# Start of a fused attention and gated-MLP kernel: state loads placed first, five weight loads fetched at once, and two sign steps moved

## Chip, cores, metric

One core of one Trainium2 chip. The metric is the time of one execution in microseconds (us), several executions each; "span" is the same execution as the profiler sees it, some 1.8 us shorter. This is a program on one core, so no other core's clock plays a part.

## The reference

```python
def _attn_ref(x, state):            # x (8, 8, 512, 64), state (8, 8, 32, 64), float32
    scores = scale * x @ state^T;  softmax -> a;   xread = a @ state
    scores2 = scale * state @ x^T; softmax -> a2;  sread = a2 @ x
    return concatenate([xread, sread], axis=2)

def _moe_ref(x, w_in, w_out):       # x (4608, 512) after the bridge; w_in (512, 2048)
    h = x @ w_in
    return (h * cos(h)) @ w_out
```

(`^T` and the softmax line are shortened.) The weights arrive as 64-bit floats. The kernel loads them raw and converts them on the chip; a good part of its first 125 us is this conversion.

## The kernel before: what the change touches

The start loads the first batch's x (eight loads, one per head) and half of the state, and asks for the first three weight loads. The two hardware queues are those of SP (`nc.sync`) and ScalarE (`nc.scalar`); Pool (`nc.gpsimd`) has the software queue.

```python
    def load_x(b, queues):
        src = x[b].rearrange("h (c p) d -> p c h d", p=P)
        for h in range(H):
            queues[h % 2].dma_start(out=x_b[:, :, h], in_=src[:, :, h])
    # ... cut ...
    load_x(0, (nc.sync, nc.scalar))
    # ... cut ...
    load_state(0, (nc.scalar, nc.gpsimd))      # eight loads of 32 KB, four each
    # ... cut ...
    fetch(3)                                   # weight loads 0, 1, 2, 512 KB each
    load_state(1, (nc.sync, nc.sync))
    warm(2, at[0])
    a0 = attn[0] = Attention(0)
    a0.all_tokens()                            # 16 transposes of x, four copies
    states(0, at[0])                           # 4 transposes of the state
    states_kept(0, at[0])
    a0.scores()
    warm(6, acc[SIDE][1])                      # matmuls nobody reads
    convert(0, "12ab")
    convert(1, "12a")
    a0.max1()                                  # two L305 reductions
    a0.spread1()
    a0.shift()
    a0.exp1()
    convert(0, "cd")
    convert(1, "bcd")
    a0.sums()
    a0.spread1()
    convert(2, "12")
    a0.norm1()
    # ... products, max2, exp2, then the regular steps, each a hidden tile with a gate
```

One weight load is converted in six steps. "1" and "2" are ScalarE's (the high and the low word as float), "a" and "b" are VectorE's (Pool does "a" of load 1). "c", the **sign step**, is VectorE's L226: it takes two operands from SBUF and frees the raw data. "d" is Pool's sum (L236). Raw data sits in three slots, and load n + 3 waits until load n's "c" is through.

## Time and profile before

| kernel before | us |
|---|---|
| time, median of six executions | 821.08 (820.25 to 821.51) |
| last x load landed | 8.4 |
| last state load of the first half landed | 12.39 |
| first weight load landed | 9.8 |
| first reduction of max1 began | 16.54 |
| norm1 ended | 27.45 |
| copy of the first gate (L445) began | 31.88 |
| first L389 of the stage's end (below: "stage end") | 121.64 |
| TensorE holds the path from about | 125 |

Terms: a load has *landed* when its completion is recorded. max1, exp1, sums and norm1 are the steps of the first softmax, max2 and exp2 the start of the second; the *gate* is h * cos(h) of a hidden tile, and its first step copies h. TensorE's clock is called *cold* where only half of it was granted (0.50) and *warm* at the full one (1.00).

The landings are from the trace's records of each load's completion, the landmarks below them from the chain of waits and the timeline. The lines of the chain are in the prediction.

### The profile page before, as it was taken

Reading aid. Unit: us, or ns where it says so; the run is one execution under the profiler, and the core shown is the slowest. Engines: PE = TensorE matmul, PEld = TensorE weight load, DVE = VectorE, ACT = ScalarE, POOL = GpSimd, SP = SyncE. Lnnn points to the kernel's source line nnn. Section 1 sums busy time; section 2 is a strip of 40 time slices with the busy share of each in tenths; the row PEclk is TensorE's granted clock in tenths of the full one; section 3 lists DMA queues with packets and bytes.
Section 4 is the critical chain, followed back from the end, with each engine's and each line's share of the span. In section 5 each row is a group of like instructions: output and inputs, shape, how many; then the busy total and the mean of one; then the engine's idle time right before and its main releaser. Section 6 shows DMA issues by size and latency. Waiting matters only on the chain.

```text
span 818.6 us, 7603 instructions
## 1 busy us (share of the span) xinstructions
PE 779.7 (95%) x2736; PEld 349.9 (43%) x2736; DVE 435.0 (53%) x671; ACT 397.6 (49%) x644; POOL 184.0 (22%) x135
## 2 busy tenths in 40 slices
PE   6788788989999999999999999999999999999997
PEld 3233234334434443444444344444344444455554
DVE  3899897653355435863454456743554355432431
ACT  2667775554447444644455444634473445322222
POOL 2244237876100000154000000451000002620200
PEclk7899999999999999999999999999999999999999
DMA  6575350101000211030010211120000112100021
GB/s 154 180 213 178 123 155 1 26 8 45 1 15 12 52 26 26 13 65 0 1 26 7 58 23 16 33 46 0 14 14 0 27 26 54 75 1 13 14 38 38
DMA packets 111653, 37.19 MB, mean 45 GB/s; under 512 B 103616, under 2 KB 103616, under 8 KB 111616
## 3 DMA queue, kind: packets, MB, share of 16 engines
q1 hardware_dynamic: 108800, 35.93, 18.1%
q10 hardware_dynamic: 2688, 0.66, 0.4%
q8 instruction: 21, 0.34, 0.2%
q0 software_dynamic: 128, 0.13, 0.1%
q14 instruction: 16, 0.13, 0.1%
HBM read 27.79 MB, written 8.91 MB: 45 GB/s over the span
## 4 chain that ended last, share of the span: by engine, by line
PE 78%; DVE 11%; ACT 7%; issue 1%; DMA 1%; POOL 0%; ACTq 0%; DVEq 0%; POOLq 0%
PE o L504 42%; PE h L439 25%; PE at L291 4%; PE o L621 3%; DVE q L448 2%; PE at L378 2%; ACT q L454 1%; PE at L264 1%; DVE g_all L460 1%; ACT q L453 1%; DVE xT L311 1%; DVE aT L355 1%; ACT xT L337 1%; DVE w_in L226 1%; DVE w_in L221 1%
## 5 line engine op out<-in xcount | busy, mean ns | idle before, releaser
L439 PE MATMUL h<-aT,sw 128*128 128x512 f32 x512 | 247.8, 607 | 16.4 <-DVE g_all L460 11.9
L504 PE MATMUL o<-g_all,w_out 128*128 128x512 f32 x512 | 238.7, 603 | 4.5 <-DVE sw L418 2.9
L466 POOL TENSOR_TENSOR g_all<-g_all 128x512 f32<-128x512 f32 x80 | 112.0, 1421 | 460.7 <-DVE g_all L460 455.7
L445 ACT ACTIVATE q<-h 128x512 f32<-128x512 f32 (+1 forms) x144 | 82.2, 571 | 270.2 <-PE h L439 270.2
L448 DVE SCALAR_TENSOR_TENSOR q<-q,h 128x512 f32<-128x512 f32 (+1 forms) x144 | 94.2, 654 | 208.8 <-ACT q L445 208.8
L504 PE MATMUL o<-g_all,s 128*128 128x512 f32 x384 | 177.3, 598 | 0.0
L460 DVE TENSOR_TENSOR g_all<-h,q 128x512 f32<-128x512 f32 (+1 forms) x144 | 94.8, 658 | 139.5 <-ACT q L454 139.3
L439 PEld LDWEIGHTS h<-aT,sw 128*128 128x128 f32 x512 | 98.0, 194 | 145.5 <-issue 112.1
L504 PEld LDWEIGHTS o<-g_all,w_out 128*128 128x128 f32 x512 | 93.9, 190 | 127.1 <-issue 120.6
L453 ACT ACTIVATE q<-q 128x512 f32<-128x512 f32 (+1 forms) x144 | 87.5, 608 | 103.7 <-DVE q L448 103.7
L504 PEld LDWEIGHTS o<-g_all,s 128*128 128x128 f32 x384 | 70.3, 190 | 88.4 <-issue 83.6
L454 ACT ACTIVATE q<-q,halfpi 128x512 f32<-128x512 f32 (+1 forms) x144 | 100.5, 698 | 4.5
L236 POOL TENSOR_TENSOR w_out<-w_out,s 128x512 int32<-128x512 int32 x20 | 27.2, 1379 | 84.8 <-DVE w_out L226 80.0
L466 DVE TENSOR_TENSOR g_all<-g_all 128x512 f32<-128x512 f32 x48 | 33.2, 692 | 1.6
L439 PE MATMUL h<-sT,w_in 128*128 128x256 f32 x128 | 30.2, 379 | 0.0
L236 POOL TENSOR_TENSOR w_in<-w_in,s 128x512 int32<-128x512 int32 x16 | 21.7, 1369 | 37.7 <-DVE w_in L226 37.7
L420 ACT COPY sw<-at 128x512 f32<-128x512 f32 x48 | 25.7, 588 | 9.0 <-PE at L291 9.0
L621 PE MATMUL o<-w_out,g_all 128*128 128x512 f32 x64 | 29.6, 592 | 0.0
L439 PEld LDWEIGHTS h<-sT,w_in 128*128 128x128 f32 x128 | 24.3, 190 | 10.1 <-issue 6.7
L510 DVE SCALAR_TENSOR_TENSOR held<-o,held 128x512 f32<-128x512 f32 x40 | 25.4, 681 | 3.7 <-PE o L504 3.7
L291 PE MATMUL at<-w_in,stT 64*32 64x512 f32 x384 | 26.1, 601 | 0.0
L531 DVE STREAM_TRANSPOSE ot<-held 128x512 f32<-128x512 f32 x32 | 22.2, 694 | 0.0
(84 smaller groups left out, 472.5 us busy)
## 6 DMA issues: line engine op xcount, KB each, us to landing
out_dram<-ot SPq DMA_DIRECT2D x136, 64.0 KB, 2.0
g_all<-in_moe_w_out_dram SPq DMA_DIRECT2D x8, 1024.0 KB, 5.0
x_b<-in_x_dram SPq DMA_DIRECT2D x60, 128.0 KB, 2.9
g_all<-in_moe_w_in_dram SPq DMA_DIRECT2D x6, 1024.0 KB, 5.2
g_all<-in_moe_w_in_dram SPq DMA_DIRECT2D x4, 512.0 KB, 5.6
x_b<-in_moe_w_out_dram SPq DMA_DIRECT2D x1, 1024.0 KB, 5.7
xT<-in_moe_w_out_dram SPq DMA_DIRECT2D x1, 1024.0 KB, 7.8
x_b<-in_x_dram ACTq DMA_DIRECT2D x4, 128.0 KB, 4.7
```

Source lines behind the costliest of these rows:

```text
L236: nc.gpsimd.tensor_tensor(bits[:, r], bits[:, r], e.bitcast(I32)[:, r], op=ALU.add)
L291: nc.tensor.matmul(out=(to or at)[j][Ns * k:Ns * k + Ns, 0:n], lhsT=w[D * j:D * j + D, self.b, Ns * k:Ns * k + Ns], rhs=r(slice(D * j, D * ...
L420: nc.scalar.copy(dst, to[j][:, 0:c1 - c0])
L439: nc.tensor.matmul(out=t.hp, lhsT=t.lhs(i), rhs=t.rhs(i), start=(i == 0), stop=(i == t.kn - 1))
L445: nc.scalar.activation(t.q, t.hp, func=ACTF.Copy, bias=MAGIC)
L448: nc.vector.scalar_tensor_tensor(out=t.q, in0=t.q, scalar=MAGIC, in1=t.hp, op0=ALU.subtract, op1=ALU.subtract)
L453: nc.scalar.activation(t.q, t.q, func=ACTF.Abs)
L454: nc.scalar.activation(t.q, t.q, func=ACTF.Sin, bias=halfpi, scale=-TWO_PI)
L460: nc.vector.tensor_tensor(t.g, t.hp, t.q, op=ALU.mult)
L466: engine.tensor_tensor(out, a, b, op=ALU.subtract)
L504: nc.tensor.matmul(out=acc[bank][ch], lhsT=w[:, i, P * ch:P * ch + P], rhs=g.g, start=(i == 0), stop=(i == NH - 1))
L621: nc.tensor.matmul(out=acc[MAIN][i], lhsT=t.g[:, P * i:P * i + P], rhs=w_out[:, :, t.f, :], start=(n == 0), stop=(n == NF - 1))
```

## The change

Its intent: put the state first on its queue, as the scores waited for it; have the weights in early; and keep two VectorE steps away from Pool's use of the same memory.

```diff
-    load_x(0, (nc.sync, nc.scalar))
+    load_x(0)                    # all eight on nc.sync
@@ fetch: places of the raw data
-                at_ = n_fetched % 3
+                at_, c0 = (n_fetched - 2) % 3, 0
+                if n_fetched < 4:     # loads 0..3: two halves of two slots
+                    at_, c0 = n_fetched // 2, n_fetched % 2 * 2 * m * w
@@ convert
-        if "c" in parts and i + 3 < N_LOADS:
-            fetch(i + 4)
+        if "c" in parts and i not in (1, 2) and i + 3 < N_LOADS:
+            fetch(max(i + 4, 6))
-        e = low[i % 2][:, 0:m * w]...
+        c0 = m * w if i in (2, 3) else 0
+        e = low[i % 2][:, c0:c0 + m * w]...
@@ start
-    fetch(3)
+    fetch(5)
-    a0.all_tokens()
+    a0.all_tokens(0, 3)
     states(0, at[0])
     states_kept(0, at[0])
+    a0.all_tokens(3, 4)
     a0.scores()
-    warm(6, acc[SIDE][1])
+    warm(7, acc[SIDE][1])
@@
-    convert(0, "cd")
     convert(1, "bcd")
     a0.sums()
+    convert(0, "cd")
```

(Cut: the new arguments of `all_tokens` and the call for later batches. The changed kernel's lines are numbered four or so higher: L305 becomes L309, L226 becomes L230, L445 becomes L449.)

More of the change, by code (lines that the diff above doesn't have):

```diff
@@ L102, with load_x @@
     stT = consts.tile([P, B, P], F32)
-    def load_x(b, queues):
+    def load_x(b):
         src = x[b].rearrange("h (c p) d -> p c h d", p=P)
         for h in range(H):
-            queues[h % 2].dma_start(out=x_b[:, :, h], in_=src[:, :, h])
+            nc.sync.dma_start(out=x_b[:, :, h], in_=src[:, :, h])
     zeros = g_all[:, 0]
     nc.vector.memset(zeros, 0.0)
-    load_x(0, (nc.sync, nc.scalar))
+    load_x(0)
     st_src = state.rearrange("b (k j) n d -> j k n b d", j=2)
@@ L181, in fetch @@
                 m, w = dst.shape[1:]
-                at_ = n_fetched % 3
+                at_, c0 = (n_fetched - 2) % 3, 0
+                if n_fetched < 4:
+                    at_, c0 = n_fetched // 2, n_fetched % 2 * 2 * m * w
                 if n_fetched >= N_LOADS:
                     at_ = 3 + n_fetched - N_LOADS
-                raw = raw_at[at_].bitcast(I32)[:, 0:2 * m * w]
+                raw = raw_at[at_].bitcast(I32)[:, c0:c0 + 2 * m * w]
                 raw = raw.rearrange("p (m f) -> p m f", m=m)
@@ L211, in convert_part @@
         m, w = dst.shape[1:]
-        e = low[i % 2][:, 0:m * w].rearrange("p (m f) -> p m f", m=m)
+        c0 = m * w if i in (2, 3) else 0
+        e = low[i % 2][:, c0:c0 + m * w].rearrange("p (m f) -> p m f", m=m)
         if p == "1":
@@ L273, in tokens_kept, with all_tokens @@
             nc.scalar.copy(self.xT[:, k], at[k % 2])
-        def all_tokens(self):
+        def all_tokens(self, k0, k1):
             xp = [acc[k // 2][k % 2] for k in range(NK)]
-            for k in range(NK):
+            for k in range(k0, k1):
                 for c in range(NC):
@@ L429, in part @@
         if (name, args) == ("reads", (1,)) and b + 1 < B:
-            load_x(b + 1, (nc.sync, nc.sync))
+            load_x(b + 1)
     class Tile:
```

## The prediction

> **What bounds the kernel now.** I read the page first: the busy digits by slice, then the chain that ended last.
>
> ```profile
> PE   6788788989999999999999999999999999999997
> ...
> DVE  3899897653355435863454456743554355432431
> ...
> PEclk7899999999999999999999999999999999999999
> ```
>
> One slice is 20.5 us. TensorE stands at 90% or more from the ninth slice on; in slices 2 to 6 VectorE is the fuller one. So the kernel is a start, a VectorE-bound stage to about 125 us, and then TensorE to the end. The changed lines are all in the first 30 us. They leave the work behind that alone, so what they can give is one constant shift. I therefore read the chain of waits over the first 32 us in order of time (columns: start us, length us, what):
>
> ```profile
> 1.85 5.22 DMA x_b<-in_x_dram
> ...
> 7.09 0.32 ACTq L123
> ...
> 7.45 4.94 DMA s<-in_state_dram
> ...
> 12.52 1.10 PE at L138 x4
> ...
> 14.49 2.06 PE at L291 x16
> 16.54 1.31 DVE m L305 x2
> ...
> 20.44 0.60 DVE w_in L226
> 21.04 0.35 DVE w_in L223
> ...
> 21.41 1.65 DVE w_in L226
> 23.06 1.23 DVE m L305 x2
> ...
> 26.22 1.23 DVE aT L355
> ...
> 31.88 0.49 ACT q L445
> ```
>
> The path to the scores (L291) is not x but the state: ScalarE's queue issues four x loads and only then its four state loads, and these come late. The timeline of the first 60 us gives the issues:
>
> ```profile
> 0.72 2.21 ACTq L108 DMA_DIRECT2D x_b<-in_x_dram  x4
> ...
> 4.18 3.71 ACTq L123 DMA_DIRECT2D s<-in_state_dram  x4
> ...
> 8.43 0.66 PE L264 MATMUL o<-ident,x_b 128*128 128x128 f32 x4 [0.66 <-DMA x_b<-in_x_dram]
> ...
> 12.52 1.09 PE L138 MATMUL at<-ident,s 128*128 128x128 f32 x4 [3.43 <-DMA s<-in_state_dram]
> ```
>
> Its 3.71 us for four issues of about 0.35 us are waits: eight completion semaphores go round the two hardware queues, and each state load waits for an x load that holds its semaphore. The last one waits for the x load that landed at about 7.1, is issued at 7.45 and lands at 12.39, behind 512 KB weight loads in the same engines. The last x was there at 8.4, so TensorE stood idle 3.43 us for the state alone, then ran the transposes and scores on a cold clock (1.00 of the clock granted in 0 to 5 us, 0.50 in 10 to 15).
>
> **What the Trainium skill says.** "DMA: Bandwidth & Descriptors", section "Issuing engines are not separate DMA queues": loads of all issuers run on the same 16 engines and interleave; issuing from several only saves issue time. The trace agrees: an ACT state load of 32 KB took about 4.9 to 6.7 us to land here, while the SP state loads issued from 9 to 14 us have a median of 2.3. "SBUF — State Buffer", section "Who interferes with whom": a VectorE operation with two SBUF inputs contends with a GpSimd operation that reads SBUF, a reduction does not. The trace agrees: one sign step (L226, 128x512) took 0.68 us alone and 1.65 us beside Pool's sum of 21.12 to 22.50, and the L305 reductions took 1.29 us for two beside the next Pool sum, against 1.31 without. "ScalarE: Activation LUTs", section "What ACT_TABLE_LOAD costs": about 1283 ns for the load; the trace has 1.28 us at 7.92, between ScalarE's last issue and its first copy. "TensorE: Matmul & The Clock Gate", section on the clock gate: half clock after an idle window of some 3.4 us; the trace's half-clock transposes at 12.52 (0.42 us mean against 0.27) follow such a gap.
>
> **The change, part by part.**
>
> *State first, x on SP alone.* ScalarE now issues its four state loads at once, from 0.7, without a wait. They should land at about 3.0 to 4.5 (2.3 us for such a load in a quiet stretch, some more behind x). Pool's four are as before; the last was issued at 3.3 and landed at about 8.6 and I take 8.0 now, as one hardware queue competes with it instead of two. SP issues eight x loads: four at 0.5 us each to 2.8, then one after each landed holder of its semaphore (first state about 3.1, first x about 4.0, second state, second x about 4.7), so the last goes out at about 5.0 and, at 3 to 3.4 us, lands at about 8.3. Bytes agree: x landed at one 128 KB load per 0.55 us in the quiet stretch, and ten such units (x and half the state) from 2.9 make 8.4. So x is no earlier; the state no longer adds 4 us. With the state's transposes ahead of the last of x: state transposed 8.0 to 8.7, last x 8.7 to 9.35, its copy (0.69) to 10.1, scores of the last head pair end at about 10.5. Before: 16.5. The table load goes to about 2.3, out of the way.
>
> *Weights.* Their loads now stand behind all of x on SP. The first is issued at about 5.5 instead of 3.77 and lands after x at about 9.8 (512 KB at the 300 to 340 GB/s of the weights' stretches is some 1.6 us; before it landed at about 9.8 also), the second at about 11.5 (before 11.9). The first conversion is ahead of the maxima in VectorE's order: ScalarE 9.85 to 10.5, VectorE's two steps (0.42 + 0.43) to 11.45. That, not the scores, becomes the wait: max1 starts at 11.5 instead of 16.52. **Gain 5.0 us.** Loads four and five were issued at 21.1 and 23.1 and used at 25.75 and 32.25 with no wait for a DMA named in the timeline, so having them early is worth nothing by itself; the loads afterwards keep their distance.
>
> *Sign steps.* Before, from the end of shift (20.44) to the start of sums (23.0) VectorE ran 0.68 + 0.42 + 1.65 us. Now exp1 (1.06 on ScalarE) covers the second load's two steps (0.43 + 0.69, Pool idle), sums start 1.1 us after shift, and the first load's sign step (0.69) stands after them, when Pool's sum (1.3) is over. So 2.55 becomes 1.1 + 0.7 = 1.8: **gain 0.75 us**. VectorE's norm1 ends at 11.5 + (27.45 - 16.52) - 0.75 = 21.7, 5.75 earlier. The other branch: Pool's sum of the first load starts at about 19.2, ends 20.5; 16 products (1.3) and two copies (0.65) make the first weights of the hidden layer at 22.6, against 27.59 when hidden started: 5.0 earlier only. It now comes after norm1 and is the later wait of the first hidden tile. But the tile's gate at 31.77 waited for VectorE's max2 and ScalarE's exp2, not for it: h needs 1.7 to 3.3 us from 22.6, to at most 25.9, and exp2 would end at about 26.1. So the shift of the gate is about 5.6.
>
> *A seventh warm-up matmul* adds 0.43 to 0.9 us to TensorE while it would wait for Pool: nothing on the path.
>
> Sum: 5.0 + 0.75 less 0.15 for joints = 5.6 us. Everything after is released by the work before it, with no clock of its own, so I carry it whole: 821.1 - 5.6 = 815.5; I add 0.3 for what the VectorE stage may lose in new overlaps with Pool. **815.8 us**.
>
> **Rivals.** (1) *The wait moves to the weights.* If x and the first weights fill the engines more than I count, the first 512 KB lands at 11.5 to 12 instead of 9.8; max1 then starts at about 13.5 and the gain is 3.5: 817.6. For it: the weights have lost 1.7 us at issue, and 3 MB of weights are now asked for at once. Against it: within a queue the first weights stand ahead of the rest, and x moved at only some 235 GB/s, which leaves issue and latency as the limit. (2) *Pool's sum of the first load becomes the path*: if h is later than exp2, the gain is 5.0 or less, to 816.2 or so; speaking for it is a cold TensorE, against it the shorter idle times. (3) *The clock gate or new collisions decide.* In the trace a 3.4 us half-clock window falls at about 125 to 129, just where TensorE takes over the path (the chain shows four hidden matmuls there at 3.22 us, later 1.72). A shift of the start by 5 us against a window that runs on by itself may save these 1.5 us or put them elsewhere: 814.3 to 817.3. (4) *The gain is given back in the VectorE stage.* The sign steps of later loads still run to 1.65 when they meet Pool; but nothing there was waiting for the start, so I hold it unlikely: 820 or more.
>
> **Range and chances.** Rivals 1 and 3 set the width: 813.8 to 818.2. Two per cent is 16.4 us, more than the whole time before max1 today; so within 2% at 0.98, the rest divided.
>
> **What would show it.** In the changed trace: state transposes at about 8 and named as waiting on Pool's loads or x at most; the first L305 at about 11.5 and held by the two steps of the first conversion rather than by the scores; both first sign steps near 0.69 us; sums right after exp1; the first gate's copy at about 26; and the same 5 to 6 us of lead at 125 us and at the end. I am wrong if the first L305 is not earlier than 13.5, if the first weights land after 11, or if the lead at 30 us is gone at 125.

## The result, and the profile after

The changed kernel took **814.87 us** (814.12 to 815.61, six executions), the kernel before 821.08; the ratio is 0.9926, 95% interval 0.9913 to 0.9938. Ratios here and below are the mean time of one kernel's fast runs over that of the other's in the same rounds, so not quite the ratio of the medians. The spans of the profiled executions are 818.6 and 813.0 us.

The chain of waits of the changed kernel, first 32 us (start, length, what), with the lines that answer to those shown of before:

```profile
0.72 2.63 DMA s<-in_state_dram
...
5.43 4.61 DMA g_all<-in_moe_w_in_dram
...
10.07 0.79 ACT w_in L218
...
10.88 0.44 DVE w_in L225
...
11.34 0.43 DVE w_in L227
11.77 1.23 DVE m L309 x2
...
15.62 1.06 ACT aT L336
...
16.71 1.31 DVE m L309 x2
...
18.62 0.55 DVE w_in L230
...
20.35 1.24 DVE aT L359
...
26.10 0.50 ACT q L449
```

The state is off the middle of the path; what stays of it is its first load, whose landing at 3.35 lets SP issue another x load. Then comes the first weight load, landing at 10.04, its conversion by ScalarE (L218) and VectorE (L225, L227), and at once max1 (L309): 11.77 instead of 16.54. After shift, exp1 leads straight to the sums at 16.71, and the one sign step left on the path (L230, 0.55) stands behind them. norm1 (L359) ends at 21.59 instead of 27.45, the gate's copy (L449) begins at 26.10 in the chain instead of 31.88.

The timeline of the same stretch (start, length, engine, what):

```profile
0.72 2.13 ACTq L123 DMA_DIRECT2D s<-in_state_dram  x4
...
0.73 4.66 SPq L108 DMA_DIRECT2D x_b<-in_x_dram  x8
...
5.43 2.66 SPq L190 DMA_DIRECT2D g_all<-in_moe_w_in_dram  x5
...
8.17 0.60 PE L138 MATMUL at<-ident,s 128*128 128x128 f32 x4
...
15.96 0.69 DVE L230 SCALAR_TENSOR_TENSOR w_in<-g_all,w_in 128x512 int32<-128x512 int32 x1
...
16.80 1.28 POOL L240 TENSOR_TENSOR w_in<-w_in,s 128x512 int32<-128x512 int32 x1 [3.01 <-ACT aT L336]
```

ScalarE's four state issues now run together; their loads landed between 3.35 and 6.14. All eight x loads are issued by 5.4, the five weight loads right behind them. The state's transposes start at 8.17, before the last of x landed at 8.68. The second load's sign step takes 0.69 us where it took 1.65, and is over before Pool's sum starts at 16.80.

The lead through the run: 4.77 us at max1, 5.78 at the gate, 5.51 at the stage end (121.64 against 116.13), 5.6 in the spans (818.6 less 813.0). So almost nothing is given back.

### The profile page after: what moved, and what is told of

Its sections match the earlier page's. It is cut to its first block, busy times and chain, and to the rows that moved or that the text cites. A ratio compares the mean times of both kernels' runs of the same rounds, so it can differ in the third digit from the quotient of the medians.

```text
span 813.0 us, 7602 instructions
## 1 busy us (share of the span) xinstructions
PE 778.6 (96%) x2738; PEld 349.3 (43%) x2738; DVE 434.5 (53%) x671; ACT 398.3 (49%) x644; POOL 183.4 (23%) x135
## 4 chain that ended last, share of the span: by engine, by line
PE 78%; DVE 11%; ACT 8%; issue 1%; DMA 1%; POOL 0%; SPq 0%; DVEq 0%; POOLq 0%; ACTq 0%
PE o L508 42%; PE h L443 25%; PE at L295 4%; PE o L625 3%; DVE q L452 2%; PE at L382 2%; ACT q L458 1%; PE at L268 1%; DVE g_all L464 1%; ACT q L457 1%; DVE xT L315 1%; DVE aT L359 1%; DVE w_in L225 1%; ACT xT L341 1%; ACT aT L336 1%
## 5 line engine op out<-in xcount | busy, mean ns | idle before, releaser
L449 ACT ACTIVATE q<-h 128x512 f32<-128x512 f32 (+1 forms) x144 | 82.2, 571 | 269.3 <-PE h L443 269.3
L443 PEld LDWEIGHTS h<-sT,w_in 128*128 128x128 f32 x128 | 24.3, 190 | 10.1 <-issue 6.7
```

Source lines behind the costliest of these rows:

```text
L443: nc.tensor.matmul(out=t.hp, lhsT=t.lhs(i), rhs=t.rhs(i), start=(i == 0), stop=(i == t.kn - 1))
L449: nc.scalar.activation(t.q, t.hp, func=ACTF.Copy, bias=MAGIC)
```

## Experiments

All ran beside the kernel before. Times alone settle little here: single runs of one version spread over 1.3 to 2.7 us (7.3 in x_two_queues), and an interval is about 0.0025 wide, some 2 us. The landmarks from the profiles settle more. For each run: first reduction of max1, the gate's copy, both as the chain has them, the first L389 (or its counterpart) of the stage's end, and the time. Each landmark is from one profiled execution.

| run | max1 | gate | gate less max1 | stage end | time us (n) | ratio to before (95%) |
|---|---|---|---|---|---|---|
| before | 16.54 | 31.88 | 15.34 | 121.64 | 821.08 (6) | |
| after | 11.77 | 26.10 | 14.33 | 116.13 | 814.87 (6) | 0.9926 (0.9913 to 0.9938) |
| sign_back | 12.09 | 27.42 | 15.33 | 117.24 | 816.50 (5) | 0.9947 (0.9935 to 0.9959) |
| late_fetch | 11.84 | 26.17 | 14.33 | 116.97 | 814.96 (5) | 0.9932 (0.9920 to 0.9944) |
| order_back | 12.01 | 26.41 | 14.40 | 116.37 | 815.40 (6) | 0.9939 (0.9926 to 0.9952) |
| only_queues | 13.09 | 28.42 | 15.33 | 118.24 | 817.64 (5) | 0.9956 (0.9945 to 0.9968) |
| clock_kept | 11.72 | 26.05 | 14.33 | 115.86 | 814.78 (4) | 0.9933 (0.9918 to 0.9947) |
| after_again | 11.77 | 26.11 | 14.34 | 116.89 | 815.90 (4) | 0.9940 (0.9928 to 0.9953) |
| weights_behind | 14.39 | 28.72 | 14.33 | 118.54 | 818.13 (4) | 0.9972 (0.9958 to 0.9987) |
| only_sign | 16.02 | 30.38 | 14.36 | 121.06 | 819.56 (4) | 0.9985 (0.9972 to 0.9997) |
| x_two_queues | 22.07 | 36.47 | 14.40 | 127.33 | 824.58 (6) | 1.0042 (1.0020 to 1.0065) |
| clock_kept_more | 11.72 | 26.04 | 14.32 | 115.78 | 814.22 (5) | 0.9923 (0.9910 to 0.9936) |
| after_third | 12.58 | 26.98 | 14.40 | 116.79 | 815.13 (5) | 0.9932 (0.9920 to 0.9944) |
| two_queues_late_w | 14.73 | 29.06 | 14.33 | 119.08 | 817.69 (5) | 0.9968 (0.9954 to 0.9982) |

The column "gate less max1" falls into two groups: 15.33 and 15.34 with the old order of the sign steps, 14.32 to 14.40 with the new. So the gain is a sum of two parts that don't touch each other: when max1 starts, and 1.0 us of sign steps.

**sign_back**: the sign steps in their old order, on the changed kernel.

```diff
+    convert(0, "cd")
     convert(1, "bcd")
     a0.sums()
-    convert(0, "cd")
```

(The fetch that follows load 0's "c" is moved to load 1's, as both share a slot.)

> The changed kernel with the first two sign steps in their old order (first load's, then the second's, then the sums). Contention theory: the second sign step meets Pool's sum of the first load and takes about 1.65 us again instead of 0.69, so the sums start 1.7 us later after shift and norm1, with the first load's step no longer behind the sums, ends about 1.0 us later than in the changed kernel; first gate at about 27.0 instead of 26.0; time about 815.9. Rival, order alone without contention: 0.69 us for both steps, only 0.1 us later, time 814.9 to 815.0.

Chain of waits of sign_back (start, length, what):

```profile
15.91 0.60 DVE w_in L230
...
16.88 1.65 DVE w_in L230
18.53 1.23 DVE m L309 x2
```

and from its timeline, Pool's sum of the first load:

```profile
16.59 1.39 POOL L240 TENSOR_TENSOR w_in<-w_in,s 128x512 int32<-128x512 int32 x1 [2.49 <-DVE w_in L230]
```

The second step, beside that sum, takes 1.65 us again and from max1 to the gate it is 1.00 us more. The contention theory holds, the rival (order alone, 0.1 us) falls. The gate is 1.3 us later than in the changed kernel, not 1.0, as the first weights happened to land at 10.47 in this execution.

**only_sign**: the same part alone, on the kernel before.

```diff
-    convert(0, "cd")
     convert(1, "bcd")
     a0.sums()
+    convert(0, "cd")
@@ convert
-        if "c" in parts and i + 3 < N_LOADS:
-            fetch(i + 4)
+        if "c" in parts and i != 1 and i + 3 < N_LOADS:
+            fetch(max(i + 4, 5))
```

> The kernel before with one edit: the second load's sign step ahead of the first's, which goes behind the sums (and the fetch of loads 3 and 4 moved behind it). Contention theory: both steps 0.69 us, norm1 ends 1.0 us earlier after max1 than in the kernel before (9.9 instead of 10.9 us after its start), first gate 0.7 to 1.0 us earlier, time about 820.0. Rival, the products of the first load now wait for Pool and the gate is no earlier: 820.8.

Max1 to gate is 14.36 instead of 15.34, so 0.98 us, as in the full change. (The gate came 1.50 us earlier in all; the other 0.52 is an earlier max1, which the edit doesn't touch: the last of the state landed at 11.87 instead of 12.39. At the stage end this execution was 0.58 us ahead; gate to stage end varies by about 1 us between profiles of one kernel, see below.) Loads 3 and 4 were issued at 23.6 and 24.1 here, in the trace's issue records, and landed at 27.3 and 29.9; the gate did not wait for them.

**only_queues**: the other large part alone, on the kernel before.

```diff
-    load_x(0, (nc.sync, nc.scalar))
+    load_x(0, (nc.sync, nc.sync))
```

> The kernel before with one edit: all x loads on SP, so that ScalarE's queue starts with the state. My theory: state lands by 7, first weights at about 10, max1 at about 11.9; sign steps collide as before; first gate about 4.5 us earlier than in the kernel before (27.3), time about 816.6, three quarters of the whole gain. Rival, the parts need each other (weights fetched three at a time arrive late, or the state's place in TensorE's order holds it): under 3 us, 818 or more.

The gate came 3.5 us earlier, not 4.5; the time moved by the ratio 0.9956, some 3.6 us. The last x landed at 8.98 and the first weights at 10.33, each 0.3 us later than in the changed kernel, but max1 began at 13.09: with the state's transposes behind x's the scores started at 11.2, and in this execution they took 1.88 us on a cold clock.

```profile
11.21 1.88 PE at L291 x16
```

So this one line is about three fifths of the gain at the gate (3.46 of 5.78). It does two things at once: the state's issues no longer wait for x loads to land, and its loads no longer run beside the weights on the other queue. No run separates the two.

**order_back**: the state's transposes behind x's, on the changed kernel.

```diff
-    a0.all_tokens(0, 3)
+    a0.all_tokens(0, 4)
     states(0, at[0])
     states_kept(0, at[0])
-    a0.all_tokens(3, 4)
```

> The changed kernel with the state's transposes behind all of x's. My theory: scores end 0.6 us later, at about 11.9, but the first conversion's two steps hold max1 to 11.7 anyway, so max1 starts only 0.2 us later; time about 815.1. Rival, the scores are the bound: max1 0.6 to 0.8 us later, time 815.6.

Chain of waits of order_back:

```profile
10.82 1.19 PE at L295 x16
12.01 1.30 DVE m L309 x2
```

Max1 began at 12.01, 0.24 us later, and the scores, not the weights, now released it. So the order of the transposes is worth about 0.2 us when the clock is warm, because the conversion of the first weights holds max1 anyway. Together with a cold clock it can be more (only_queues), and I have no run that tells that part apart.

**late_fetch**: three weight loads at the start, the others later, in the new places.

```diff
-    fetch(5)
+    fetch(3)
     load_state(1, (nc.sync, nc.sync))
```

> The changed kernel with loads 3 and 4 (of five) asked for only with the sixth, at about 19.2 us, in their new places. My theory: prefetch was never waited for; load 3 lands at about 23, its first conversion starts 0.7 us late on ScalarE, which has 1.1 us of slack before exp2: first gate at 26.0 plus or minus 0.2, time 814.9 plus or minus 0.3. Rival, early fetch carries part of the gain: gate over 0.7 us later, time 815.6 or more.

The edit did less than I meant. The new places are free from the start, so SP had nothing to wait for and issued loads 3 and 4 at 13.8 and 14.3, behind the state, instead of 7.0 and 7.6; they landed at 17.7 and 20.2 instead of 14.2 and 17.0. Max1 to gate is 14.33, the time 814.96: no difference. Together with only_sign, where the two landed ten microseconds later than that (its gate is 4.2 us later) without holding the gate, this shows that fetching five at once brings nothing by itself up to the gate. At the stage end this execution was 0.8 us behind the changed kernel, but its TensorE clock was halved from 42 to 49 us, and the unchanged kernel did the same in after_again.

**weights_behind**: is the first weights' landing really what max1 waits for?

```diff
-    fetch(5)
     load_state(1, (nc.sync, nc.sync))
+    fetch(5)
```

> The changed kernel with the second half of the state (eight 32 KB loads) ahead of the five weight loads on SP. My theory: the first weights' landing is what max1 waits for; they are issued some 4 us later and land at about 13 to 14 instead of 10.0, max1 starts at about 15 instead of 11.8, first gate 3 us later, time about 818. Rival, the scores or VectorE's own work are the bound and the weights only happen to land then: max1 under 1 us later, time under 816.

Chain of waits of weights_behind:

```profile
9.21 3.56 DMA g_all<-in_moe_w_in_dram
...
14.39 1.23 DVE m L309 x2
```

The first weights landed at 12.77, 2.7 us later than before the edit, max1 began 2.62 us later, the gate 2.62 us later. The rival (scores or VectorE's work as the bound) falls. They were issued at 9.21, as late as expected, but then took only 3.56 us to land, against 4.61 when x stood ahead of them, so landing and max1 came a little before my figures (13 to 14, and 15).

**x_two_queues**: x on two queues as in the kernel before, but behind the state.

```diff
-    load_x(0)
     load_state(0, (nc.scalar, nc.gpsimd))
+    load_x(0, nc.scalar)         # odd heads on ScalarE's queue
```

> The changed kernel with the odd heads of x on ScalarE's queue again, but behind the state loads. My theory (bytes and latency bind, not the issuer; what mattered is the state's place): the last x lands at 8.7 to 9.5, as its issue waits for a completion semaphore, the first weights at 9.5 to 10.3; max1 starts at 11.7 to 12.4, first gate at 26.0 to 26.7, time within 0.6 of the changed kernel. Rival, one queue for x is itself the gain: max1 over 1.5 us later.

My theory fell by ten microseconds. Chain of waits of x_two_queues:

```profile
5.45 13.01 DMA x_b<-in_x_dram
...
22.07 1.31 DVE m L310 x2
```

The last x load was issued at 5.45 and landed at 18.46. SP, with four x loads fewer, issued the first weights at 3.33, and from then on ScalarE's x loads shared the engines with 3 MB of weights from the other queue: the weight loads landed at 9.2, 11.4, 13.1, 14.7 and 18.25, and the last x just behind the last of them. From 6 to 14 us ScalarE's queue moved 1740 packets and 0.43 MB, SP's 1100 packets and 2.28 MB: more packets, but a fifth of the bytes, as x has rows of 256 bytes and the weights of 2 KB and 4 KB. That the length of the rows is the reason fits these counts; no run varied it. It is the only version slower than the kernel before. One of its six executions took 818.86 us, the others 824.5 to 826.2; I have no profile of that one.

**two_queues_late_w**: the same split of x, with the weights asked for later.

```diff
     (x_two_queues)
-    fetch(5)
     load_state(1, (nc.sync, nc.sync))
+    fetch(5)
```

> The kernel with the odd heads of x on ScalarE's queue (whose last x landed at 18.5 beside 3 MB of weights on the other queue) and the second half of the state ahead of the weights on SP, so that the weights are asked for some 5 us later. Contention theory (the two queues share the engines, and 256-byte rows lose to 2 KB rows): most of x is through before the weights start, the last x lands at 8.5 to 11, max1 starts at 14 to 16 as with the state ahead of the weights on one queue (14.4), time 817.5 to 819.5. Rival, a split of x over two queues is slow by itself: last x after 14, time over 821.

Chain of waits of two_queues_late_w:

```profile
3.34 4.12 DMA x_b<-in_x_dram
...
9.27 3.85 DMA g_all<-in_moe_w_in_dram
...
14.73 1.23 DVE m L310 x2
```

The last x landed at 9.21, and max1 again waited for the weights (13.12). So the split was not slow by itself; it was slow beside the weights on the other queue. One queue for x and weights is what lets the early fetch of five stand behind x instead of beside it. One execution of the kernel before took 1351.84 us at a mean clock of 0.557; it counts as slow and is left out.

**clock_kept**: three matmuls that nobody reads, in TensorE's wait before the first hidden tile of the second batch.

```diff
+        if step == NF:
+            for _ in range(3):
+                nc.tensor.matmul(out=at[1], lhsT=w_in[:, 0, 0:P],
+                                 rhs=w_in[:, 0, 0:S], start=True, stop=True)
         hidden(t)
```

> The changed kernel plus three matmuls that nobody reads, in TensorE's wait ahead of the first hidden tile of the second batch (116.6 to 119.4 in the trace of the changed kernel), so that the wait is not idle. Clock theory: the half-clock window at 119 to 122.5, which made four hidden matmuls take 3.5 us instead of 1.7, does not occur; runs of this kernel lie closer together, near 813.2, some 0.8 to 1.7 us below the changed kernel. Rival, the window falls there for another reason: no change, 814.9; or, if the added 2.6 us outlast the wait, 0.3 us slower.

> The changed kernel unchanged, as the measure for the others on this chip: 814.9 plus or minus 0.5, gate of the first tile at 26.0 to 26.6; single runs spread over 1.5 us by whether a half-clock window falls at about 119.

At the place where TensorE takes over the path, the chain of waits of the kernel before had

```profile
124.86 3.22 PE h L439 x4
```

and that of the changed kernel, for the same four hidden matmuls and a later set of four,

```profile
119.36 3.51 PE h L443 x4
...
125.91 1.72 PE h L443 x4
```

Both kernels pay the half clock there. The timeline of TensorE, changed kernel:

```profile
114.76 1.88 PE L508 MATMUL o<-g_all,w_out 128*128 128x512 f32 x4
119.36 3.51 PE L443 MATMUL h<-aT,sw 128*128 128x512 f32 x4 [2.72 <-DVE g_all L464]
```

and clock_kept:

```profile
114.72 1.88 PE L508 MATMUL o<-g_all,w_out 128*128 128x512 f32 x4
116.43 2.74 PE L806 MATMUL at<-w_in 128*128 128x512 f32 x6
119.08 1.98 PE L443 MATMUL h<-aT,sw 128*128 128x512 f32 x4
```

With the wait filled, the hidden matmuls take 1.98 us in the timeline instead of 3.51 (2.90 in after_again). That alone would not show that the fill did it, as five of the twelve profiles without it kept the full clock there too (sign_back, order_back, only_queues, weights_behind and two_queues_late_w).

The clock records of the traces settle it. In each execution the clock changes only at steps of 3.41 us, and where these steps lie differs from one execution to the next. Cut a trace at the steps: over the fourteen traces, whenever TensorE was busy for less than 1.54 us of a stretch at full clock, the next stretch had half the clock (52 of 52); between 1.54 and 1.9 us it was so in 14 of 47, above that in none of 3000. The stretch with this wait had 0.7 to 1.2 us of work in the seven unfilled executions that lost the clock and 1.6 to 1.8 in the five that kept it. Without the fill, by my estimate from the traces, it would have had 1.4 us in clock_kept (its last matmul before the fill ended at 116.60, the stretch ran from 115.17 to 118.58) and 0.9 in clock_kept_more. So both would have lost the clock. In the executions without the fill, where the steps lie against the wait decides, not the version. The median, 814.78, is 1.1 us under the changed kernel's of the same call, but not near the 813.2 that I expected, and the runs did not lie closer together (813.89 to 815.86); the intervals overlap. after_again missed its figure too: 815.90 against 814.9 plus or minus 0.5.

**clock_kept_more**: the same, with ten instead of seven warm-up matmuls in the start.

```diff
-    warm(7, acc[SIDE][1])
+    warm(10, acc[SIDE][1])
```

> The kernel with the three matmuls in the later wait, and ten instead of seven warm-up matmuls in the start. The first hidden tiles' passes take 0.43 us instead of 0.85 for want of the half-clock window at 20 to 27, but VectorE's max2 and exp2 release the first gate: gate at 26.0 to 26.6 as before; no half-clock window at 119; time about 1 us below the changed kernel of the same call. Rival, h releases the gate (my prediction's second rival): gate earlier by over 0.3 us.

> The changed kernel unchanged, for comparison with the other two on this chip: 815.0 plus or minus 0.8, gate at 26.0 to 26.6.

The granted clock stayed full to 30 us. The first eight hidden matmuls ran from 21.69 to 25.39 instead of 22.14 to 27.95 in clock_kept, and the gate's copy began at 26.04 instead of 26.05. So it is not h that releases the gate, and more warm-up matmuls (the change added one, which has no run of its own) move nothing there. The median was 814.22 against 815.13 for the changed kernel. The version with the filled wait was about 1 us ahead; that is the best version seen, shown for the four matmuls by the traces, not established for the whole kernel by the times, whose intervals overlap.

after_third shows the same lottery in the start. In its profiled execution the second and the third four transposes of x took 1.08 us each instead of 0.68 and 0.63, and the chain reads

```profile
10.77 1.82 PE at L295 x16
12.58 1.31 DVE m L309 x2
```

so the scores ran on until 12.58 and max1 waited for them, 0.8 us later than in the other two profiles of this kernel, where the weights were last; the gate came at 26.98, outside the 26.0 to 26.6 that I expected. The balance between the two waits is that close.

## Why the prediction was right

The time was put at 815.8 us in a range of 813.8 to 818.2; the three sets of runs gave 814.87, 815.90 and 815.13. That is a gain of 5.3 us foreseen and of 6.1, 4.9 and 5.6 measured, by the ratios. That the middle of these is so near is partly luck: of the terms of the sum, max1 fell short by 0.23 us and the sign steps gave 0.25 more. The steps, one by one:

- *The state is what the scores wait for; putting it first removes that.* Right (only_queues). In detail, the last state load of before did not itself wait for the x load that landed at 7.07: the third one did, and the last stood behind it on ScalarE's queue. The last of the state landed at 6.99, earlier than my 8.0, and the last x at 8.68, later than my 8.3. Scores ended at 11.3, not 10.5: after the last x copy (10.2, foreseen 10.1) they took another 1.1 us, not 0.4. None of this reached the path in the profile of the changed kernel.
- *The first weights' landing becomes the wait, at 9.8, and max1 starts at 11.5.* Right: 10.04 and 11.77. That max1 moves by what the landing moves was then shown by weights_behind. The gain was 4.77 of the 5.0 foreseen. The rival in which the weights land at 11.5 to 12 did not occur.
- *The sign steps give 0.75 us.* The mechanism was right and the size short: 1.00, in three comparisons. My sum began both intervals at the end of shift and took 2.55 to 1.8; the chain has 2.62 before and 1.66 after (1.11 up to the sums and 0.55 that the moved step adds), so 0.96 of the 1.0.
- *Five loads at once bring nothing by themselves.* Right up to the gate, by late_fetch and only_sign.
- *The gate is released by max2 and exp2, not by h.* Right: the hidden matmuls began at 22.18, the gate's copy right behind exp2 at 26.00 (timeline; 26.10 in the chain), and clock_kept_more moved the first without moving the second.
- *The shift is carried whole.* Right: 5.78 at the gate, 5.6 at the end. The loss at the stage end of 0.27 is smaller than the spread between the three profiles of the changed kernel (gate to stage end is 89.8 to 90.8 us).
- *The clock window at 125 us may be hit or missed.* Right as a source of spread; the change didn't decide it. But the window is not a thing apart that the start is shifted against: in seven executions it follows the wait, wherever that lies (119 us after the change, 125 before), and only the steps of 3.41 us run on by themselves. Three readings were wrong, and nothing in the sum rested on them. The full clock that I read for the first 5 us does not fit the warm-up matmuls there, 1.06 us each against 0.59 later; the trace has no clock record before 6.0 us. The half clock of the transposes at 12.52 did not come of the gap of 3.43 us before them: it was granted from 9.42, when the gap had only begun at 9.09. And TensorE stands at 90% from the tenth slice on, not the ninth.

What I had not seen is why x went to one queue. I counted x through one queue as no loss; the run that I expected to be equal, with x on two behind the state, reached max1 ten microseconds later.

## What to carry to other kernels

When the path of a start runs through a small load, look at what stands ahead of it in its queue and which completion it must wait for before it is issued; and put a large load that is not yet needed behind the small ones on the same queue, not beside them on another. Before taking a small change's time for its worth, split it at landmarks in the trace: here one interval fell into two groups in fourteen profiles, 1.0 us apart, while single times of one version spread over 1.3 to 2.7 us. A VectorE step with two SBUF operands (1.65 us beside Pool's sum, 0.69 alone) is worth an order that keeps the two apart.

## What the Trainium skill lacked or had wrong

- "DMA: Bandwidth & Descriptors", section "Issuing engines are not separate DMA queues": it says that issuing from several engines only saves issue time. Here the choice of queue moved the last x landing from 8.68 to 18.46 us and the time from 814.9 to 824.6 us. The same page's section "Queues, rings and completion order" has a reason that fits, round-robin between queues packet by packet; what it lacks is the consequence, that a queue of short rows (256 bytes here) falls behind one of long rows (2 KB and more): 0.43 MB against 2.28 MB from 6 to 14 us.
- "TensorE: Matmul & The Clock Gate", section on the clock gate: the free-running window of about 3.4 us agrees with the traces (half-clock stretches of 3.4, 6.8 and 10.2 us). It lacks how little work in a window loses the clock: here less than 1.54 us in 3.41 always did (52 of 52), 1.54 to 1.9 us sometimes (14 of 47), more never. And it lacks what the phase then does in the middle of a kernel: the same four hidden matmuls took 1.98, 2.90, 3.51 and 3.53 us in clock_kept and in three executions of the changed kernel, and the scores 1.19 us on a warm clock (order_back) or 1.88 on a cold one (only_queues).
- "SBUF — State Buffer", section "Who interferes with whom": it agrees. The sign step took 0.69 us alone and 1.65 beside Pool's sum, and the gate moved by 1.00.
- "ScalarE: Activation LUTs", section "What ACT_TABLE_LOAD costs": the load itself agrees (1.28 us), but the drain of about 1380 ns that the section adds for every switch does not show: in the changed kernel the load stands from 28.17 to 29.45, the activation before it ends at 28.15 and the one after it begins at 29.46, so the whole switch is 1.31 us.
